# First two token tiles of a two-branch attention kernel: loaded by rows on one DMA queue and turned by TensorE, instead of transposed by DMA

## The chip, the cores and the metric

The kernel runs on one core of one Trainium2 chip (trn2). The metric is the device time of one execution in microseconds (us); 'span' is the part of it from the first to the last instruction in the profile. The kernel before takes 486.67 us (median of 3 runs, 486.44 to 487.22).

## The reference, cut to what matters

```python
def reference(A_x, A_wqkv, A_wo, B_x, B_wqkv, B_wo, gate_w):   # x: [1, 2048, 1024] bf16, wqkv: [1024, 3072]
    def _A_ref(x, wqkv, wo): ...      # linear attention, 32 heads of 32
    def _B_ref(x, wqkv, wo):          # sliding window of 8 keys, dilation 2
        qkv = (x @ wqkv).reshape(B, S, 3, H, Dh) ...
        ...
    x = A_x                           # both branches read the same x
    g = _sigmoid((x * gate_w).sum(-1, keepdims=True))
    return g * _A_ref(x, A_wqkv, A_wo) + (1 - g) * _B_ref(x, B_wqkv, B_wo)
```

The kernel starts with the value projection of branch B: `x @ wqkv[:, 2048:3072]`, a [2048 x 1024] by [1024 x 1024] product. The kernel's matmuls sum over the partitions, in eight blocks of 128 features, so they take x with its features on the partitions, that is, transposed. This document is about the first 16 us, in which that product begins.

## The kernel before

Every operation is recorded with an engine, a guessed cost and a priority. A list scheduler written in Python then fixes the order of each engine's instructions before compilation. Waits are on semaphores, one semaphore for each load. x is cut into 16 token tiles of 128 tokens (256 KB each). The weights of this product come in two halves of 512 columns, each as four "pairs" of 128-row blocks (256 KB a pair).

```python
WARM = 11
...
def load_x(t, prio):                       # DMA transpose: HBM rows -> SBUF, features on partitions
    return P.op("sp", lambda e: e.dma_start_transpose(xT[:, :, t*128:(t+1)*128], x2[e_, r*128:(r+1)*128, :]), 1.5, ...)

def load_w(slot, half, src, c0, prio, d0=0, d1=8, eng="sp", after=()):   # blocks d0..d1 of one half
    return P.op(eng, lambda e: e.dma_start(ws[slot][:, d0:d1, half*512:half*512+512], src[:, d0:d1, c0:c0+512]), ...)

load_x(0, 0)
load_w(0, 0, Bw, 2048, 0.1, 0, 2, "act")   # pairs 1 and 2 on ScalarE's queue
load_w(0, 0, Bw, 2048, 0.2, 2, 4, "act")
load_w(0, 0, Bw, 2048, 0.3, 4, 6)          # pairs 3 and 4 on the sync queue
load_w(0, 0, Bw, 2048, 0.4, 6, 8)
for t in range(1, NT):
    load_x(t, 3 + t)
for d in range(0, 8, 2):                   # the second half
    load_w(0, 1, Bw, 2560, 6.1 + 0.1 * d, d, d + 2)
...
for i in range(WARM):                      # matmuls on zeros, to get TensorE's clock up
    P.op("pe", lambda e: e.matmul(banks[7].ap(), warm[:, 0:128], warm[:, :], start=True, stop=True), 0.43, ..., prio=-1)
...
for t, half in [...]:                      # tiles 0-3 half 1, tiles 0-3 half 2, tiles 4-7 half 1, ...
    step = 2 if t == 0 else 8              # tile 0 waits for its weights pair by pair
    for d in range(0, 8, step):
        o = group(bank, xs, w, [xr, ws[0].part((d, d+step), ...)], d, d + step)   # 8 matmuls 128x512 in all
    move(...)                              # PSUM -> SBUF on ScalarE or VectorE
    P.op("sp", ... e.dma_start(vB_hbm[...], vt[...]) ...)                          # store the values
```

So the early loads come from two queues: tile 0 and pairs 3 and 4 from the sync engine's (SP), pairs 1 and 2 from ScalarE's (ACT).

Of the kernel before, what the change touches and what calls it, by code (L numbers as in the profile page):

```python
# [6 lines left out]
ACT = mybir.ActivationFunctionType  # L7
ALU = mybir.AluOpType
AX = mybir.AxisListType
BF16 = mybir.dt.bfloat16  # L10
# [52 lines left out]
class Prog:  # L63
# [58 lines left out]
    def schedule(self, dma_rate=0.2e6):  # L122
# [6 lines left out]
        dma_free = 0.0  # L129
# [20 lines left out]
        while done < len(self.ops):  # L150
            best = None
            for e in self.ENGS:
                while wait[e] and wait[e][0][0] <= free[e]:
                    _, _, o = heapq.heappop(wait[e])
                    heapq.heappush(avail[e], (o.prio, o.seq, o))
                if avail[e]:
                    t = free[e]
                elif wait[e]:
                    t = wait[e][0][0]
                else:  # L160
                    continue
                if best is None or t < best[0]:
                    best = (t, e)
            assert best is not None, "no operation can go"
            t, e = best
            if not avail[e]:
                while wait[e] and wait[e][0][0] <= t:
                    _, _, o = heapq.heappop(wait[e])
                    heapq.heappush(avail[e], (o.prio, o.seq, o))
            _, _, o = heapq.heappop(avail[e])  # L170
            if e == "pe":

                if o.mode != mode and mode != "m":
                    near = [x for x in avail[e] if x[2].mode == mode and x[0] < o.prio + 30]
                    if near:
                        x = min(near)
                        avail[e].remove(x)
                        heapq.heapify(avail[e])
                        heapq.heappush(avail[e], (o.prio, o.seq, o))
                        o = x[2]  # L180
                if o.mode != mode:
                    t += 0.09
                mode = o.mode
            o.start = t
            o.end = t + o.cost
            free[e] = o.end
            fin = o.end
            if o.chan is not None:
                dma_free = max(dma_free, o.end) + o.lat
                fin = dma_free + o.pad  # L190
            o.pos = len(self.order[e])
            self.order[e].append(o)
            done += 1
            for u in o.users:
                lat = self.LAT[o.eng] if (u.eng != o.eng or o in u.raw) and o.chan is None else 0.0
                if u.eng == o.eng == "pe":
                    lat = 0.0
                ready_at[u] = max(ready_at[u], fin + lat)
                left[u] -= 1
                if left[u] == 0:  # L200
                    ready(u, ready_at[u])
# [915 lines left out]
def build_kernel(nc, A_x, A_wqkv, A_wo, B_x, B_wqkv, B_wo, gate_w, out):  # L1117
    del B_x
    S = A_x.shape[1]
    NT = S // 128  # L1120
    HS = S // 2
    x2 = A_x[0].rearrange("(m e) d -> e m d", e=2)
    out2 = out[0].rearrange("(m e) d -> e m d", e=2)

    base = [(nc.sbuf_base + 31) // 32 * 32]
# [40 lines left out]
    banks = [Bank(i) for i in range(8)]  # L1166
# [51 lines left out]
    warm = SB([128, 512], BF16, "warm", at=pk.t[2].lo)  # L1218
    gwb = SB([128, 1024], BF16, "gwb", at=pk.t[3].lo)
    xn = Ring([SB([128, 1024], BF16, "xn%d" % i, at=az.t[i].lo) for i in range(2)])  # L1220
    top_ = base[0]
    base[0] = ph
    osb = Ring([SB([128, 1024], BF16, "o%d" % i) for i in range(2)])
# [4 lines left out]

    FILL = 0.2
    PVLAG = 3  # L1230
    WARM = 11
    PASSES = 6
    mm = lambda n: max(n / 2400.0, 0.0267) + 0.0025
    act = lambda n: 0.19 + n / 1200.0
# [2 lines left out]
    def plan(seen):  # L1237
# [25 lines left out]
        def C(eng, fn, cost, writes, reads=()):  # L1263
            return P.op(eng, fn, cost, reads=reads, writes=writes, prio=-1)

        for z in vst.t:
            C("pool", lambda e, z=z: e.memset(z[:, :, 32:33], 1.0), 0.1, [z.part((0, 16), (32, 33))])
        C("pool", lambda e: e.memset(eps[:], 1e-6), 0.1, [eps.all()])
        for i, (n, offs) in enumerate(KINDS):
            for h, o in enumerate(offs):  # L1270
                m = mtmp[h]
                b0 = o + 64 * h
                C("pool", lambda e, m=m: e.memset(m[:], 1.0), 0.1, [m.all()])

                C("pool", lambda e, m=m, n=n, b0=b0: e.affine_select(out=m[:, :, 0:n], in_=m[:, :, 0:n], compare_op=ALU.is_ge, fill=0.0, base=b0,
                                                                     pattern=[[0, 2], [1, n]], channel_multiplier=-1), 0.3, [m.all()], [m.all()])
                C("pool", lambda e, m=m, n=n, b0=b0: e.affine_select(out=m[:, :, 0:n], in_=m[:, :, 0:n], compare_op=ALU.is_ge, fill=0.0, base=7 - b0,
                                                                     pattern=[[0, 2], [-1, n]], channel_multiplier=1), 0.3, [m.all()], [m.all()])
                C("dve", lambda e, m=m, n=n, h=h, i=i: e.tensor_copy(msk[i][64 * h:64 * h + 64, :, :], m[64 * h:64 * h + 64, :, 0:n]), 0.2, [msk[i].all()], [m.all()])
                P.ops[-1].prio = 1100  # L1280
        C("pool", lambda e: e.memset(zsel[:], 0.0), 0.3, [zsel.all()])

        C("dve", lambda e: e.memset(warm[:, :], 0.0), 0.15, [warm.all()])
# [29 lines left out]
            return P.op(eng, lambda e: e.dma_start(ws[slot][:, d0:d1, half * 512:half * 512 + 512], src[:, d0:d1, c0:c0 + 512]), 0.4 + 0.2 * n,  # L1313
                        writes=[ws[slot].part((d0, d1), (half * 512, half * 512 + 512))], prio=prio, chan="w%d_%d_%d" % (slot, half, d0), lat=0.55 * n, after=after)

        load_x(0, 0)
        load_w(0, 0, Bw, 2048, 0.1, 0, 2, "act")
        load_w(0, 0, Bw, 2048, 0.2, 2, 4, "act")
        load_w(0, 0, Bw, 2048, 0.3, 4, 6)
        load_w(0, 0, Bw, 2048, 0.4, 6, 8)  # L1320
        for t in range(1, NT):
            load_x(t, 3 + t)
        for d in range(0, 8, 2):
            load_w(0, 1, Bw, 2560, 6.1 + 0.1 * d, d, d + 2)
        P.op("sp", lambda e: e.dma_start(gwb[:, :], gate_w[None, :].to_broadcast([128, D])), 0.6, writes=[gwb.all()], prio=29, chan="gw", lat=0.8)
# [46 lines left out]
        for i in range(WARM):  # L1372
            P.op("pe", lambda e: e.matmul(banks[7].ap(), warm[:, 0:128], warm[:, :], start=True, stop=True), 0.43, reads=[warm.all()], writes=[banks[7].iv], prio=-1)


        early = {(2, 0): (1, 0, Bw, 1024, 21), (4, 1): (2, 0, Bw, 0, 22), (7, 1): (1, 1, Bw, 1536, 23), (10, 1): (2, 1, Bw, 512, 24),
                 (12, 1): (3, 0, Aw, 1024, 25), (14, 1): (3, 1, Aw, 1536, 26)}
        for t, half in [(4 * b + i, half) for b in range(NT // 4) for half in range(2) for i in range(4)]:
            vt, vs = vst.next()
            xs, xr = x_tile(t)  # L1380
            bank = main.next()
            w, wr = w_half(0, half)
            step = 2 if t == 0 else 8
            for d in range(0, 8, step):
                o = group(bank, xs, w, [xr, ws[0].part((d, d + step), (half * 512, half * 512 + 512))], d, d + step)
            move(vt[:, :, 0:32], lambda bank=bank: bank.ap().rearrange("p (h d) -> p h d", d=32), 512, bank, vt.part((0, 16), (0, 32)))
            P.op("sp", lambda e, t=t, vt=vt, half=half: e.dma_start(vB_hbm[t * 128:(t + 1) * 128, half * 528:half * 528 + 528], vt[:, :, :].rearrange("p h d -> p (h d)")), 0.6, reads=[vt.all()],
                 writes=[hb(t * 128, (t + 1) * 128, half)], chan="vst%d" % vs, lat=0.5, prio=5)
            if (t, half) in early:
                load_w(*early[t, half], after=[o])  # L1390
        load_w(0, 0, Aw, 2048, 30)
        load_w(0, 1, Aw, 2560, 31)

# [424 lines left out]
```

## Time and profile before

| what | value | where |
|---|---|---|
| time | 486.67 us | three runs |
| TensorE (PE) busy | 474.2 us of 485.2 (98%) | busy table |
| first real matmul | 5.54 us | timeline |
| waits of PE for loads after it | 0.40, 0.48, 0.16, 0.25 us | timeline, gaps beyond the normal 0.216 us from matmul to matmul |
| last pair of the second half landed | 15.02 us | landings |
| matmul that needs it (the 39th real one) | 15.08 us | its weight load at 15.06; its own record is missing from the trace |

The page of the kernel before, its busy line (engine, busy us, share of the span, instructions) and the chain that ended last by engine:

```profile
PE 474.2 (98%) x4339; PEld 222.8 (46%) x4403; DVE 285.2 (59%) x547; ACT 140.2 (29%) x227; POOL 5.9 (1%) x36
PE 95%; SPq 2%; issue 1%; DMA 1%; ACT 0%; DVE 0%
```

From 15.3 us to the end PE works without a real pause, so whatever the opening loses or gains shows one for one in the time. The timeline of PE in the opening of the kernel before (start, duration, engine, source line, operation, tiles, count, and in brackets the idle time before and who ended it). L1373 are the warm-up matmuls, L1334 the real ones:

```profile
1.25 4.01 PE L1373 MATMUL ps_all<-warm 128*128 128x512 bf16 x11 [1.25 <-DVE warm L1283]
5.54 1.47 PE L1334 MATMUL ps_all<-w,xT 128*128 128x512 bf16 x6 [0.28 <-DMA xT<-in_A_x_dram]
7.25 0.60 PE L1334 MATMUL ps_all<-w,xT 128*128 128x512 bf16 x2 [0.24 <-DMA w<-in_B_wqkv_dram]
8.17 6.82 PE L1334 MATMUL ps_all<-w,xT 128*128 128x512 bf16 x30 [0.32 <-DMA xT<-in_A_x_dram]
15.30 1.89 PE L1334 MATMUL ps_all<-w,xT 128*128 128x512 bf16 x8 [0.30 <-DMA w<-in_B_wqkv_dram]
```

Each break in the row of matmuls is ended by a load. What the loads do is seen in a table by stretch of the kernel before (columns: stretch in us; its length and the busy us of each engine with its instructions; granted clock; mean busy share of the 16 DMA engines, which can pass 1 as packets overlap; GB/s moved):

```profile
2.00:3.00 1.00, 1.00 (x4) 0.36 (x3) 0.63 (x8) 1.00 (x1) 1.00 (x6) 1.00 0.80 245
3.00:4.00 1.00, 1.00 (x4) 0.39 (x3) 0.53 (x3) 0.06 (x1) 0.79 (x5) 1.00 1.16 304
4.00:5.00 1.00, 1.00 (x5) 0.31 (x3) 0.28 (x2) 0.00 (x0) 0.90 (x5) 1.00 1.14 320
5.00:6.00 1.00, 0.72 (x5) 0.23 (x4) 0.21 (x1) 0.00 (x0) 0.89 (x5) 1.00 1.01 298
6.00:7.00 1.00, 1.00 (x5) 0.20 (x3) 0.43 (x2) 0.00 (x0) 0.41 (x2) 1.00 1.18 290
7.00:8.00 1.00, 0.62 (x3) 0.11 (x2) 0.00 (x0) 0.10 (x1) 0.00 (x0) 1.00 1.28 270
8.00:9.00 1.00, 0.83 (x4) 0.41 (x5) 0.00 (x0) 0.50 (x1) 0.00 (x0) 1.00 0.94 213
```

### The profile page before, as it was taken

How to read it: one execution, taken by the hardware profiler on the slowest of the kernel's cores; microseconds unless marked ns; L12 is line 12 of the kernel's file. 1: busy time of each engine (PE TensorE's matmuls, PEld its weight loads, DVE VectorE, ACT ScalarE, POOL GpSimd, SP SyncE). 2: the span in 40 equal slices, each digit the busy share in tenths (PEclk: the TensorE clock that was granted, in tenths of full speed). 3: DMA queues.
4: the chain of work that ended last, by engine and by line, in shares of the span. 5: the costliest groups of instructions: out<-in, count | busy, mean ns of one | idle time of the engine just before them, and what ended most of it. 6: DMA issues, size and time to landing. Idle time of an engine off the chain costs nothing.

```text
span 485.2 us, 10105 instructions
## 1 busy us (share of the span) xinstructions
PE 474.2 (98%) x4339; PEld 222.8 (46%) x4403; DVE 285.2 (59%) x547; ACT 140.2 (29%) x227; POOL 5.9 (1%) x36
## 2 busy tenths in 40 slices
PE   8999999999999999999999999999999999999997
PEld 3444444444444444454544554444444444444443
DVE  2121435888688888665666556496579236653434
ACT  2111121235322234334443333455532230111000
POOL 4000000000000000000000000000000000000000
PEclk9999999999999999999999999999999999999999
DMA  8999993132014459433222322820086018830212
GB/s 224 222 194 299 309 355 122 65 110 86 1 44 135 107 138 245 100 76 86 55 75 67 85 66 66 204 54 2 10 217 163 1 15 242 221 24 2 88 68 89
DMA packets 72951, 57.39 MB, mean 118 GB/s; under 512 B 37953, under 2 KB 60865, under 8 KB 72898
## 3 DMA queue, kind: packets, MB, share of 16 engines
q1 hardware_dynamic: 72210, 56.07, 44.3%
q8 instruction: 36, 0.59, 0.5%
q10 hardware_dynamic: 688, 0.59, 0.4%
q14 instruction: 17, 0.14, 0.1%
HBM read 34.49 MB, written 13.76 MB: 99 GB/s over the span
## 4 chain that ended last, share of the span: by engine, by line
PE 95%; SPq 2%; issue 1%; DMA 1%; ACT 0%; DVE 0%
PE ps_all L1334 78%; PE ps_all L1693 11%; PE ps_all L1463 2%; PE ps_all L1440 2%; SPq L1308 1%; DMA w<-in_B_wqkv_dram 1%; PE ps_all L1556 1%; SPq L1313 1%; PE ps_all L1638 0%; PE ps_all L1610 0%; ACT e L1341 0%; DVE o L1697 0%
## 5 line engine op out<-in xcount | busy, mean ns | idle before, releaser
L1334 PE MATMUL ps_all<-w,xT 128*128 128x512 bf16 x924 | 208.6, 379 | 4.5 <-issue 2.1
L1334 PE MATMUL ps_all<-xT,w 128*128 128x512 bf16 x745 | 166.3, 379 | 2.2 <-issue 1.4
L1334 PEld LDWEIGHTS ps_all<-w,xT 128*128 128x128 bf16 x960 | 91.2, 98 | 111.1 <-DMA w<-in_B_wqkv_dram 2.1
L1334 PEld LDWEIGHTS ps_all<-xT,w 128*128 128x128 bf16 x768 | 73.9, 98 | 88.7 <-issue 1.3
L1693 PE MATMUL ps_all<-w,qT 128*128 128x512 bf16 (+1 forms) x260 | 55.4, 372 | 0.2
L1693 PEld LDWEIGHTS ps_all<-w,qT 128*128 128x128 bf16 x264 | 25.9, 98 | 29.6
L1365 DVE CAST vst<-ps_all 128x512 bf16<-128x512 f32 x15 | 10.4, 694 | 43.5 <-PE ps_all L1334 43.5
L1448 ACT ACTIVATE E<-ps_all 128x1824 bf16<-128x1824 f32 (+1 forms) x18 | 30.4, 1689 | 13.4 <-PE ps_all L1440 13.4
L1345 DVE TENSOR_SCALAR e<-e 128x512 bf16<-128x512 bf16 x64 | 18.4, 290 | 26.9 <-ACT e L1343 14.0
L1697 DVE SCALAR_TENSOR_TENSOR o<-ps_all,gm,xT 128x512 bf16<-128x512 f32 (+1 forms) x25 | 18.0, 728 | 21.1 <-PE ps_all L1693 20.8
L1341 ACT ACTIVATE e<-ps_all 128x512 bf16<-128x512 f32 x32 | 19.1, 598 | 39.0 <-PE ps_all L1334 38.1
L1343 ACT ACTIVATE e<-ps_all 128x512 bf16<-128x512 f32 x32 | 19.1, 598 | 32.3 <-PE ps_all L1334 32.3
L1295 DVE TENSOR_TENSOR mx<-mx,kT 128x1024 bf16<-128x1024 bf16 x32 | 20.9, 688 | 10.9 <-ACT kT L1366 10.8
L1295 DVE TENSOR_TENSOR mx<-mx,qT 128x1024 bf16<-128x1024 bf16 x32 | 20.8, 687 | 7.9 <-ACT qT L1369 7.9
L1451 DVE TENSOR_TENSOR E<-E,msk 128x1824 bf16<-128x1824 bf16 (+1 forms) x18 | 19.9, 1104 | 7.8 <-ACT E L1448 7.4
L1366 ACT ACTIVATE vst<-ps_all 128x512 bf16<-128x512 f32 x17 | 10.2, 601 | 48.5 <-PE ps_all L1334 45.1
L1480 DVE TENSOR_TENSOR ot<-ps_all,rs 128x512 bf16<-128x512 f32 x36 | 23.3, 686 | 0.0
L1366 ACT ACTIVATE az<-ps_all 128x512 bf16<-128x512 f32 x22 | 13.2, 601 | 34.5 <-PE ps_all L1334 34.5
L1366 ACT ACTIVATE kT<-ps_all 128x512 bf16<-128x512 f32 x20 | 11.9, 597 | 37.6 <-PE ps_all L1334 37.6
L1347 DVE SCALAR_TENSOR_TENSOR pk<-ps_all,e 128x512 bf16<-128x512 f32 x32 | 22.0, 689 | 0.7
L1369 ACT ACTIVATE qT<-ps_all 128x512 bf16<-128x512 f32 x19 | 11.4, 598 | 37.4 <-PE ps_all L1334 37.3
L1369 ACT ACTIVATE xT<-ps_all,g 128x512 bf16<-128x512 f32 x10 | 6.9, 689 | 45.1 <-PE ps_all L1334 45.1
(72 smaller groups left out, 260.2 us busy)
## 6 DMA issues: line engine op xcount, KB each, us to landing
rb<-rc_hbm SPq DMA_DIRECT2D x32, 256.0 KB, 5.2
w<-in_A_wqkv_dram SPq DMA_DIRECT2D x6, 1024.0 KB, 9.0
v<-vB_hbm SPq DMA_DIRECT2D x36, 132.0 KB, 2.7
vB_hbm<-vst SPq DMA_DIRECT2D x32, 132.0 KB, 6.2
w<-in_B_wqkv_dram SPq DMA_DIRECT2D x4, 1024.0 KB, 9.5
xn<-in_A_x_dram SPq DMA_DIRECT2D x16, 256.0 KB, 2.7
out_dram<-o SPq DMA_DIRECT2D x15, 256.0 KB, 2.1
oB_hbm<-ot SPq DMA_DIRECT2D x36, 96.0 KB, 2.2
```

The lines of the kernel that those rows point to most:

```text
L1295: P.op("dve", lambda e, m=m, op=op: e.tensor_tensor(m[:, 0:n], m[:, 0:n], src, op), 0.08 + n / 1920.0, reads=[m.all(), reg], writes=[m.all()],
L1334: last = e.matmul(bank.ap(), lhs(dc), rhs(dc), start=(dc == 0), stop=(dc == 7))
L1341: P.op("act", lambda e: e.activation(e_[:, :], bank.ap(), ACT.Exp), act(512), reads=[bank.iv], writes=[e_.all()])
L1343: P.op("act", lambda e: e.activation(e_[:, :], bank.ap(), ACT.Exp, accum_out=qe[:, col:col + 1]), act(512) + 0.1, reads=[bank.iv], writes= ...
L1345: P.op("dve", lambda e: e.tensor_scalar(e_[:, :], e_[:, :], 1.0, 1e-6, op0=ALU.min, op1=ALU.add), 0.25, reads=[e_.all()], writes=[e_.all()])
L1347: P.op("dve", lambda e: e.scalar_tensor_tensor(out=dst, in0=bank.ap(), scalar=0.0, in1=e_[:, :], op0=ALU.max, op1=ALU.add), dps(512), read ...
L1366: fa = lambda e: e.activation(dst, src(), ACT.Copy)
L1369: fa = lambda e: e.activation(dst, src(), ACT.Copy, scale=scale)
L1448: P.op("act", lambda e: e.activation(E[:, 0:32 * nq].rearrange("p (j q) -> p j q", j=4), ps[:, 4:8, 0:8 * nq], ACT.Exp), act(32 * nq), rea ...
L1451: P.op("dve", lambda e: e.tensor_tensor(ev(), ev(), m[:, :, :].rearrange("p r q -> p (r q)")[:, None, :].to_broadcast([128, 16, 2 * nq]), ...
L1480: P.op("dve", lambda e, r=r, bv=bv, h=h: e.tensor_tensor(o[:, 512 * h:512 * h + 512].rearrange("p (k i c) -> p k i c", k=2, c=32), bv()[:, ...
L1693: last = e.matmul(bank.ap(0, f1 - f0), qT[:, dc, t * 128:(t + 1) * 128], ws[3][:, dc, f0:f1], start=(dc == 0), stop=(dc == 7))
```

## The change

Its intent is to start real work sooner. The first two DMA transposes took the sync engine 1.38 and 1.25 us to issue and landed 4.7 and 4.8 us after their issue began. The change loads the first two tiles as plain rows, in order of need with the weight pairs, all on the sync queue. TensorE turns them with an identity matrix into PSUM, and VectorE and ScalarE copy them to where the transposes would have put them. Five warm-up matmuls go (eleven become four plus two), because the turns keep PE busy too, and the building of the masks moves behind the first projections.

```diff
+    rows_ = [SB([128, 1024], BF16, "rows%d" % i, at=az.t[2 + i].lo) for i in range(2)]
+    ident = SB([128, 128], BF16, "ident", at=er.t[0].lo)
-    WARM = 11
+    WARM = 4
+    WARM2 = 2
@@ the masks: built with priority -1 at the start before, now recorded after the projections @@
@@ the loads @@
-        load_x(0, 0)
-        load_w(0, 0, Bw, 2048, 0.1, 0, 2, "act")
-        load_w(0, 0, Bw, 2048, 0.2, 2, 4, "act")
-        load_w(0, 0, Bw, 2048, 0.3, 4, 6)
-        load_w(0, 0, Bw, 2048, 0.4, 6, 8)
-        for t in range(1, NT):
-            load_x(t, 3 + t)
+        due(load_rows(0, 0, 512, 0), 0.4, 2.0)            # due(load, issue cost, guessed landing): for the scheduler
+        due(load_w(0, 0, Bw, 2048, 0.1, 0, 2), 0.45, 2.7)
+        due(load_rows(0, 512, 1024, 0.2), 0.45, 3.1)
+        due(load_w(0, 0, Bw, 2048, 0.3, 2, 4), 0.45, 3.9)
+        due(load_rows(1, 0, 1024, 0.4), 0.45, 4.7)
+        due(load_w(0, 0, Bw, 2048, 0.5, 4, 6), 0.45, 5.5)
+        due(load_w(0, 0, Bw, 2048, 0.6, 6, 8), 0.45, 6.3)
+        for t in range(2, NT):
+            o = load_x(t, 3 + t)
@@ after the warm-ups @@
+        for t, p in [(t, p) for t in range(2) for p in range(4)]:
+            b = banks[3 + p]
+            def turn(e, t=t, b=b, p=p):
+                for k in range(2):
+                    d = 2 * p + k
+                    last = e.matmul(b.ap(128 * k, 128 * k + 128), rows_[t][:, d * 128:(d + 1) * 128], ident[:, :], start=(k == 0), stop=(k == 1), skip_group_check=True)
+                return last
+            P.op("pe", turn, 0.22, ...)
+            ...                                           # then a copy 128x256 to xT, VectorE for even p, ScalarE for odd p
+        for i in range(WARM2):
+            P.op("pe", ...)                               # two more warm-ups, as before
-            step = 2 if t == 0 else 8
+            step = 2 if t == 0 or t == 1 and half == 0 else 8
```

(Cuts are marked with "..." and "@@".) The lists of instructions, compared engine by engine, show that PE's order differs only in the opening. On the sync queue the fourth pair of the second half now comes after the first store.

More of the change, by code (lines that the diff above doesn't have):

```diff
@@ L188, in schedule @@
             if o.chan is not None:
-                dma_free = max(dma_free, o.end) + o.lat
-                fin = dma_free + o.pad
+                if o.lat is None:
+                    fin = max(o.end + 1.2, o.pad)
+                else:
+                    dma_free = max(dma_free, o.end) + o.lat
+                    fin = dma_free + o.pad
             o.pos = len(self.order[e])
@@ L1264, in C @@
             return P.op(eng, fn, cost, reads=reads, writes=writes, prio=-1)
+        C("pool", lambda e: e.memset(ident[:, :], 0.0), 0.1, [ident.all()])
+        C("pool", lambda e: e.affine_select(out=ident[:, :], in_=ident[:, :], compare_op=ALU.not_equal, fill=1.0, base=0, pattern=[[-1, 128]], channel_multiplier=1), 0.3,
+          [ident.all()], [ident.all()])
         for z in vst.t:
@@ L1268, in plan @@
         C("pool", lambda e: e.memset(eps[:], 1e-6), 0.1, [eps.all()])
-        for i, (n, offs) in enumerate(KINDS):
-            for h, o in enumerate(offs):
-                m = mtmp[h]
-                b0 = o + 64 * h
-                C("pool", lambda e, m=m: e.memset(m[:], 1.0), 0.1, [m.all()])
-                C("pool", lambda e, m=m, n=n, b0=b0: e.affine_select(out=m[:, :, 0:n], in_=m[:, :, 0:n], compare_op=ALU.is_ge, fill=0.0, base=b0,
-                                                                     pattern=[[0, 2], [1, n]], channel_multiplier=-1), 0.3, [m.all()], [m.all()])
-                C("pool", lambda e, m=m, n=n, b0=b0: e.affine_select(out=m[:, :, 0:n], in_=m[:, :, 0:n], compare_op=ALU.is_ge, fill=0.0, base=7 - b0,
-                                                                     pattern=[[0, 2], [-1, n]], channel_multiplier=1), 0.3, [m.all()], [m.all()])
-                C("dve", lambda e, m=m, n=n, h=h, i=i: e.tensor_copy(msk[i][64 * h:64 * h + 64, :, :], m[64 * h:64 * h + 64, :, 0:n]), 0.2, [msk[i].all()], [m.all()])
-                P.ops[-1].prio = 1100
         C("pool", lambda e: e.memset(zsel[:], 0.0), 0.3, [zsel.all()])
@@ L1314, in load_w, with load_rows, due @@
                         writes=[ws[slot].part((d0, d1), (half * 512, half * 512 + 512))], prio=prio, chan="w%d_%d_%d" % (slot, half, d0), lat=0.55 * n, after=after)
-        load_x(0, 0)
-        load_w(0, 0, Bw, 2048, 0.1, 0, 2, "act")
-        load_w(0, 0, Bw, 2048, 0.2, 2, 4, "act")
-        load_w(0, 0, Bw, 2048, 0.3, 4, 6)
-        load_w(0, 0, Bw, 2048, 0.4, 6, 8)
-        for t in range(1, NT):
-            load_x(t, 3 + t)
+        def load_rows(t, lo, hi, prio):
+            return P.op("sp", lambda e: e.dma_start(rows_[t][:, lo:hi], x2[0, t * 128:(t + 1) * 128, lo:hi]), 0.45, writes=[rows_[t].part((lo, hi))], prio=prio, chan="xr%d_%d" % (t, lo))
+        def due(o, cost, at):
+            o.cost, o.lat, o.pad = cost, None, at
+        due(load_rows(0, 0, 512, 0), 0.4, 2.0)
[7 more added lines that the diff above has]
+            o = load_x(t, 3 + t)
+            if t < 4:
+                due(o, 1.4, 7.6 + 1.3 * (t - 2))
         for d in range(0, 8, 2):
@@ L1373, in plan @@
             P.op("pe", lambda e: e.matmul(banks[7].ap(), warm[:, 0:128], warm[:, :], start=True, stop=True), 0.43, reads=[warm.all()], writes=[banks[7].iv], prio=-1)
+        for t, p in [(t, p) for t in range(2) for p in range(4)]:
[5 more added lines that the diff above has]
+                return last
+            P.op("pe", turn, 0.22, reads=[rows_[t].part((256 * p, 256 * p + 256)), ident.all()], writes=[b.iv], prio=-0.5 + 0.01 * p)
+            src = lambda b=b: b.ap(0, 256).rearrange("p (k s) -> p k s", k=2)
+            dst = xT[:, 2 * p:2 * p + 2, t * 128:(t + 1) * 128]
+            fn = (lambda e, dst=dst, src=src: e.activation(dst, src(), ACT.Copy)) if p % 2 else (lambda e, dst=dst, src=src: e.tensor_copy(dst, src()))
+            P.op("act" if p % 2 else "dve", fn, act(256) if p % 2 else dps(256), reads=[b.iv], writes=[xT.part((2 * p, 2 * p + 2), (t * 128, (t + 1) * 128))], prio=3 + 0.01 * p)
+        for i in range(WARM2):
+            P.op("pe", lambda e: e.matmul(banks[7].ap(), warm[:, 0:128], warm[:, :], start=True, stop=True), 0.43, reads=[warm.all()], writes=[banks[7].iv], prio=-0.4)
         early = {(2, 0): (1, 0, Bw, 1024, 21), (4, 1): (2, 0, Bw, 0, 22), (7, 1): (1, 1, Bw, 1536, 23), (10, 1): (2, 1, Bw, 512, 24),
@@ L1382, in plan @@
             w, wr = w_half(0, half)
-            step = 2 if t == 0 else 8
+            step = 2 if t == 0 or t == 1 and half == 0 else 8
             for d in range(0, 8, step):
-                o = group(bank, xs, w, [xr, ws[0].part((d, d + step), (half * 512, half * 512 + 512))], d, d + step)
+                o = group(bank, xs, w, [xT.part((d, d + step), (t * 128, (t + 1) * 128)), ws[0].part((d, d + step), (half * 512, half * 512 + 512))], d, d + step)
             move(vt[:, :, 0:32], lambda bank=bank: bank.ap().rearrange("p (h d) -> p h d", d=32), 512, bank, vt.part((0, 16), (0, 32)))
@@ L1390, in plan @@
                 load_w(*early[t, half], after=[o])
+        for i, (n, offs) in enumerate(KINDS):
+            for h, o in enumerate(offs):
+                m = mtmp[h]
+                b0 = o + 64 * h
+                P.op("pool", lambda e, m=m: e.memset(m[:], 1.0), 0.1, writes=[m.all()])
+                P.op("pool", lambda e, m=m, n=n, b0=b0: e.affine_select(out=m[:, :, 0:n], in_=m[:, :, 0:n], compare_op=ALU.is_ge, fill=0.0, base=b0,
+                                                                     pattern=[[0, 2], [1, n]], channel_multiplier=-1), 0.3, writes=[m.all()], reads=[m.all()])
+                P.op("pool", lambda e, m=m, n=n, b0=b0: e.affine_select(out=m[:, :, 0:n], in_=m[:, :, 0:n], compare_op=ALU.is_ge, fill=0.0, base=7 - b0,
+                                                                     pattern=[[0, 2], [-1, n]], channel_multiplier=1), 0.3, writes=[m.all()], reads=[m.all()])
+                P.op("dve", lambda e, m=m, n=n, h=h, i=i: e.tensor_copy(msk[i][64 * h:64 * h + 64, :, :], m[64 * h:64 * h + 64, :, 0:n]), 0.2, writes=[msk[i].all()], reads=[m.all()])
         load_w(0, 0, Aw, 2048, 30)
```

## The prediction

> **What bounds the kernel now.** TensorE. The busy table gives PE 474.2 of 485.2 us (98%) and the chain of waits is 95% PE. From 15.3 us on the chain is an almost unbroken row of 128x512 matmuls, one per 0.216 us. PE's instruction list in the changed kernel differs only in the opening, so only the first 15 us should change.
>
> **The opening now (timeline, DMA landings).** 11 warm-up matmuls on PE from 1.25 to 5.26 us. The first real matmul starts at 5.54, when the first transposed token tile lands (issued 0.80, landed 5.49; its first weight pair, on the other queue, landed 3.58). Then PE waits 0.40 us for the fourth weight pair (landed 7.21), 0.48 for tile 1 (8.13), and about 0.4 in all for the last two pairs of the second weight half (14.34 and 15.02). That is 1.3 us of stalls after 5.54. The DMA runs near 300 GB/s in 3 to 9.5 us, with a hole around 9.5 to 10.3 us because the sync queue was still issuing transposes (1.25 to 2.27 us each) and gave out the second half only at 8.31 to 10.4.
>
> **What the change does.** Two transposes (1.38 + 1.25 us of queue time) become three plain loads (about 0.5 us each); the two weight issues of the ScalarE queue move to the sync queue. 16 128x128 matmuls and 8 copies of 128x256 (estimate 0.4 us each, from 0.69/0.60 us for 128x512) are added; PE loses five warm-up matmuls.  The bytes to load are the same, so the supply still sets the pace: I estimate (0.8 to 0.9 us per 256 KB, from the old landings) half a row tile at 3.1 us, weight pairs at about 3.7, 4.9, 6.4, 7.4, tiles 2 and 3 at 8.5 and 9.6.
>
> First real matmul: 4.6 to 5.0 us. Tiles 0 and 1 share each weight pair, so when the fourth pair lands at about 7.4 only 8 matmuls remain: done at 9.2, against 10.1 for the first two tiles before. Then 22 matmuls lead to the last pair of half two at about 14.0, where before it was reached at 15.06. That pair is now issued after the first store, at about 10 us as before, so it lands at 13.5 to 14.5 and may itself take back some of the gain. All of that is on the critical path: a gain of 0.3 to 1.3 us.
>
> **Against it.** The Trainium skill ("TensorE: Matmul & The Clock Gate", Part 1) says that the clock opens only after about 3.4 us of activity, judged in a free-running window. The trace agrees: warm-ups 0.427 us apart up to 4.2 us, then 0.216. With four plus two warm-ups and gaps, the clock may open a window later (about 7.6 us); I estimate that this would cost at most 0.8 us.
>
> **Prediction.** 485.9 us, 0.8 us less than 486.67; 8 in 10 between 485.0 and 486.9. Faster by over 2%: 0.01; within 2%: 0.97; slower by over 2%: 0.02.
>
> **What would show it.** Timeline: first 128x512 matmul of weights at 4.6 to 5.0 us. Waits: the wait for tile 1 gone, waits for weight pairs early instead. Chain: unbroken PE from about 14 us instead of 15.3, with the same 470 us from there to the end. Landings: fourth pair near 7.4 us, last pair of half two before 14.5.
>
> **What would make it wrong.** The last pair of the second half landing at 15 us again (store and queue in front of it): no gain. The clock staying at half rate past 7.6 us. The fourth pair at 8 us or later. A changed split of evictions between VectorE and ScalarE that makes PE wait in the middle.

## The result, and the profile after

| | median us | range | runs |
|---|---|---|---|
| before | 486.81 | 486.44 to 487.22 | 6 |
| changed | 488.55 | 487.89 to 489.98 | 6 |

The ratio is 1.004, with a 95% interval from 1.0023 to 1.0057. Ratios here are the mean time of one kernel's fast runs over that of the other's fast runs of the same rounds, so not quite the ratio of the medians quoted. The class "within 2%" was right, but the change made the kernel slower by about 1.8 us where a gain of 0.8 was predicted, outside the stated range. Three things stand out: the changed kernel is slower, it scatters more (2.1 us against 0.8), and its time outside the span is longer (2.11 us on average against 1.74).

The same lines of the page of the changed kernel:

```profile
PE 480.4 (99%) x4414; PEld 223.5 (46%) x4414; DVE 289.0 (59%) x556; ACT 138.0 (28%) x226; POOL 6.3 (1%) x38
PE 98%; DMA 1%; SPq 0%; DVE 0%; issue 0%
```

PE's higher share is no better use: its busy time is 6.2 us longer for the same real work. (Part of that is only that fewer matmul records are missing from this trace.) The timeline of PE in the opening of the changed kernel (L1380 and L1397 warm-ups, L1389 turns, L1341 real matmuls):

```profile
1.25 1.89 PE L1380 MATMUL ps_all<-warm 128*128 128x512 bf16 x4 [1.25 <-DVE warm L1280]
3.07 0.59 PE L1389 MATMUL ps_all<-ident,rows 128*128 128x128 bf16 x4
3.45 1.06 PE L1397 MATMUL ps_all<-warm 128*128 128x512 bf16 x2
5.01 0.61 PE L1389 MATMUL ps_all<-ident,rows 128*128 128x128 bf16 x4 [0.50 <-DMA rows<-in_A_x_dram]
5.41 0.85 PE L1341 MATMUL ps_all<-w,xT 128*128 128x512 bf16 x2
6.54 0.59 PE L1341 MATMUL ps_all<-w,xT 128*128 128x512 bf16 x2 [0.28 <-DMA w<-in_B_wqkv_dram]
7.43 0.62 PE L1389 MATMUL ps_all<-ident,rows 128*128 128x128 bf16 x8 [0.30 <-DMA rows<-in_A_x_dram]
8.52 8.81 PE L1341 MATMUL ps_all<-w,xT 128*128 128x512 bf16 x40 [0.47 <-DMA w<-in_B_wqkv_dram]
```

The first real matmul comes only 0.13 us earlier than before (5.41). Only four real matmuls are done by 8.5 us, where the kernel before had started its tenth. From 8.52 on the row is unbroken and the 39th real matmul starts at 15.87 us, 0.79 us later than before; the span is 0.8 us longer (486.0). So in this execution the whole loss within the span happened before 8.52 us. The chain of waits of the changed kernel's first 16 us names the load behind it (start, duration, what):

```profile
2.70 0.47 SPq L1314
3.17 0.04 issue
3.21 5.27 DMA w<-in_B_wqkv_dram
8.48 0.05 issue
8.52 7.51 PE ps_all L1341 x34
```

It is the third weight pair: issued at 3.21, landed at 8.48. The stretches of the changed kernel:

```profile
2.00:3.00 1.00, 1.00 (x3) 0.15 (x1) 0.63 (x8) 0.09 (x1) 1.00 (x6) 1.00 0.59 179
3.00:4.00 1.00, 1.00 (x7) 0.56 (x6) 0.57 (x3) 0.30 (x1) 0.36 (x2) 1.00 0.87 304
4.00:5.00 1.00, 0.51 (x2) 0.00 (x0) 0.27 (x2) 0.08 (x1) 0.84 (x5) 1.00 0.66 183
5.00:6.00 1.00, 0.99 (x6) 0.56 (x6) 0.53 (x2) 0.34 (x1) 0.74 (x4) 1.00 0.84 272
6.00:7.00 1.00, 0.72 (x4) 0.13 (x2) 0.09 (x1) 0.04 (x1) 0.48 (x2) 1.00 0.93 305
7.00:8.00 1.00, 0.70 (x9) 0.45 (x8) 0.24 (x1) 0.13 (x1) 0.00 (x0) 1.00 1.07 273
8.00:9.00 1.00, 0.53 (x4) 0.24 (x4) 0.81 (x4) 0.53 (x2) 0.53 (x4) 1.00 1.08 160
```

Now the DMA engines idle a third of the time between 4 and 5 us (busy share 0.66, 183 GB/s), although the sync engine had issued all four pairs and both tiles by 4.16 us. In the seven stretches 1.68 MB are moved, against 1.94 before. So the loads are slower although no DMA transpose runs among them until 7 us.

A load is one semaphore raised 16 times. The Trainium skill ("DMA: Bandwidth & Descriptors", section "Why a DMA increments its semaphore by 16 and not by 1") explains that up to 16 DMA engines work on it and finish independently, and that only the full 16 mean that all data are there. This trace agrees: it holds 16 landings for each load, and in the changed kernel they lie far apart. Landing of the first and the last of the 16, in us (computed from the trace's landings; P1 to P4 are the pairs of the first half):

```
              before            changed          predicted (last)
tile 0     5.38 .. 5.49      2.53 .. 2.94 (half), 4.05 .. 4.97     3.1 (half)
P1         3.48 .. 3.58      3.68 .. 4.56          3.7
P2         5.06 .. 5.30      4.71 .. 6.41          4.9
tile 1     7.95 .. 8.13      6.02 .. 7.39
P3         6.16 .. 6.36      6.75 .. 8.48          6.4
P4         7.01 .. 7.21      7.41 .. 9.21          7.4
```

For the four pairs the first engine is close to the prediction, within 0.35 us (P4: 7.41 against 7.4). The last one, which alone counts, is 0.9 to 2.1 us later than predicted. In these loads of the kernel before, the first and the last lay within 0.25 us of each other.

### The profile page after: what moved, and what is told of

Its sections match the earlier page's. It is cut to its first block, busy times and chain, and to the rows that moved or that the text cites. A ratio compares the mean times of both kernels' runs of the same rounds, so it can differ in the third digit from the quotient of the medians.

```text
span 486.0 us, 10198 instructions
## 1 busy us (share of the span) xinstructions
PE 480.4 (99%) x4414; PEld 223.5 (46%) x4414; DVE 289.0 (59%) x556; ACT 138.0 (28%) x226; POOL 6.3 (1%) x38
## 4 chain that ended last, share of the span: by engine, by line
PE 98%; DMA 1%; SPq 0%; DVE 0%; issue 0%
PE ps_all L1341 80%; PE ps_all L1728 11%; PE ps_all L1498 2%; PE ps_all L1475 2%; DMA w<-in_B_wqkv_dram 1%; PE ps_all L1591 1%; PE ps_all L1673 0%; PE ps_all L1645 0%; SPq L1314 0%; SPq L1310 0%; DVE o L1732 0%
## 5 line engine op out<-in xcount | busy, mean ns | idle before, releaser
L1341 PE MATMUL ps_all<-w,xT 128*128 128x512 bf16 x960 | 213.1, 380 | 0.8 <-DMA w<-in_B_wqkv_dram 0.8
L1341 PE MATMUL ps_all<-xT,w 128*128 128x512 bf16 x768 | 169.0, 379 | 0.0
L1341 PEld LDWEIGHTS ps_all<-w,xT 128*128 128x128 bf16 x960 | 91.6, 98 | 109.7 <-ACT xT L1394 0.9
L1341 PEld LDWEIGHTS ps_all<-xT,w 128*128 128x128 bf16 x768 | 73.8, 98 | 88.8 <-issue 1.3
L1373 ACT ACTIVATE kT<-ps_all 128x512 bf16<-128x512 f32 x17 | 10.1, 597 | 37.2 <-PE ps_all L1341 37.1
L1465 DVE TENSOR_SCALAR qd<-qT,par 128x912 bf16<-128x912 bf16 (+1 forms) x34 | 14.6, 451 | 9.5 <-PE ps_all L1475 9.5
```

The lines of the kernel that those rows point to most:

```text
L1341: last = e.matmul(bank.ap(), lhs(dc), rhs(dc), start=(dc == 0), stop=(dc == 7))
L1373: fa = lambda e: e.activation(dst, src(), ACT.Copy)
```

## The experiments

The theories at the start were these. S: plain row loads, with no transpose between them, let the 16 engines run apart, whichever queue issues them. Q: it is the single issuing queue, as the kernel before used two. M: the moved masks get in the way of the turn copies on VectorE. C: fewer warm-ups leave TensorE's clock low for longer. Each run is set against runs of the kernel before in the same rounds; different sets of rounds ran on different chips and are compared only through these. (The expectations call the 16 engines of a load its "rings".)

### e1: two queues again

```diff
-        due(load_w(0, 0, Bw, 2048, 0.1, 0, 2), 0.45, 2.7)
+        due(load_w(0, 0, Bw, 2048, 0.1, 0, 2, "act"), 0.45, 2.7)
-        due(load_w(0, 0, Bw, 2048, 0.3, 2, 4), 0.45, 3.9)
+        due(load_w(0, 0, Bw, 2048, 0.3, 2, 4, "act"), 0.45, 3.9)
```

(The scheduler also moves the fourth pair of the second half ahead of the first store, as the sync queue is freer, and a few evictions near 60 us between ScalarE and VectorE.)

> The changed kernel with its first two weight pairs issued again on ScalarE's queue (rows stay on the sync queue). Theory S (row loads on one queue let the 16 rings of a load run apart, and PE waits for the slowest ring; what decides is plain loads without a transpose between them): spread between first and last ring of the fourth pair stays above 1 us, last ring after 8.4 us, time within 0.5 us of the changed kernel (488.5). Rival Q (the single issuing queue alone is the cause): third and fourth pair complete at 7.2 to 7.8 us, spread under 0.5 us, time 486.0 to 486.9.

Measured: 486.83 us (486.42 to 486.91), ratio to before 0.9993 (0.9979 to 1.0006). P3 landed at 6.26 .. 7.15 and P4 at 7.76 .. 7.92. The timeline of PE of e1, its last two lines before 17 us:

```profile
7.10 0.61 PE L1389 MATMUL ps_all<-ident,rows 128*128 128x128 bf16 x8
7.55 9.66 PE L1341 MATMUL ps_all<-w,xT 128*128 128x512 bf16 x43
```

The unbroken row starts at 7.55 instead of 8.52. Stretches of e1:

```profile
4.00:5.00 1.00, 1.00 (x4) 0.14 (x2) 0.78 (x3) 0.38 (x1) 0.29 (x2) 1.00 1.02 343
8.00:9.00 1.00, 1.00 (x6) 0.47 (x5) 0.73 (x3) 0.18 (x1) 0.81 (x5) 1.00 1.29 259
```

The holes are gone: 343 and 259 GB/s where the changed kernel had 183 and 160. Q's times came out, and S fell in its strong form. Q had expected a spread under 0.5 us, though, and P3 still had 0.9.

One rival was never separated from Q. A single engine issues its loads one after the other, so on one queue they are also issued later. The sync engine's issues in the changed kernel, and then those of the sync engine and of ScalarE in e1:

```profile
2.22 0.43 SPq L1310 DMA_DIRECT2D w<-in_B_wqkv_dram  x1
3.21 0.95 SPq L1310 DMA_DIRECT2D w<-in_B_wqkv_dram  x2
```

```profile
2.19 0.95 SPq L1310 DMA_DIRECT2D w<-in_B_wqkv_dram  x2
0.81 0.98 ACTq L1310 DMA_DIRECT2D w<-in_B_wqkv_dram  x2
```

P3 was issued at 3.21 in the changed kernel and at 2.19 in e1, so 1.02 us of the 1.33 by which it landed later (8.48 against 7.15) may be the later issue alone. From the start of the issue to the last landing the two kernels hardly differ: P2 4.19 us against 4.43, tile 1 4.69 against 4.64, P3 5.27 against 4.96, P4 5.52 against 5.25. Against issue time as the whole cause stands that tile 1 and P3 had been issued by 3.64 when the DMA engines of the changed kernel idled from 4 to 5 us. In all the runs below the two go together: with two queues the last pair of the first half had been issued by 2.80 to 3.31 us, with one by 4.16 to 4.33. So e1 and e2 show what moving two issues costs, and not whether the queue or the later issue is the reason.

### e2: the kernel before with one queue

```diff
-        load_w(0, 0, Bw, 2048, 0.1, 0, 2, "act")
-        load_w(0, 0, Bw, 2048, 0.2, 2, 4, "act")
+        load_w(0, 0, Bw, 2048, 0.1, 0, 2)
+        load_w(0, 0, Bw, 2048, 0.2, 2, 4)
```

> The kernel before with its first two weight pairs moved from ScalarE's queue to the sync queue, behind the first transpose; nothing else. Theory S: rings stay together behind the transpose (spread under 0.5 us for the four pairs), time rises only by the later issue, under 0.6 us. Rival Q: the one queue costs it most of what the change costs, plus 1.2 to 2 us.

Measured: 488.74 us (488.40 to 489.23), ratio 1.0036 (1.0022 to 1.0049). Moving two issues from one queue to the other, and nothing else of the change, costs as much as the whole change did. The timeline of PE of e2:

```profile
1.25 3.83 PE L1373 MATMUL ps_all<-warm 128*128 128x512 bf16 x11 [1.25 <-DVE warm L1283]
6.85 1.95 PE L1334 MATMUL ps_all<-w,xT 128*128 128x512 bf16 x6 [1.76 <-DMA w<-in_B_wqkv_dram]
```

The first real matmul waits for P1, which landed 5.20 .. 6.80 instead of 3.48 .. 3.58. Stretches of e2:

```profile
2.00:3.00 1.00, 1.00 (x4) 0.37 (x3) 0.63 (x8) 0.08 (x1) 1.00 (x6) 1.00 0.93 129
3.00:4.00 1.00, 1.00 (x4) 0.39 (x3) 0.53 (x3) 0.00 (x0) 0.79 (x5) 1.00 0.91 166
```

With the transpose alone in the early queue the DMA moves 129 and 166 GB/s where before had 245 and 304 with two queues. Here the pairs also queue up behind the transpose and are issued later (P1 at 2.23 instead of 0.80, P3 at 3.35 instead of 2.24), so this run shows the price of one queue in the kernel before; it does not show the same hole as in the changed kernel. From issue to last landing the pairs took longer too (P3 4.80 us instead of 4.12), so later issue is not all of it here.

### e3: the masks early again

The edit puts the block that builds the masks back to its old place and priority.

> The changed kernel with the masks built at the start as before. Theories S and Q: same as the changed kernel within 0.4 us (488.2 to 488.9). Rival M (mask copies moved between the turn copies on VectorE delay the opening): 0.5 us or more faster.

Measured: 489.00 us (488.08 to 489.31), ratio 1.0040. That is the changed kernel again (0.1 us above the range of 488.2 to 488.9). M is out.

### e4: eight warm-ups

```diff
-  P.op("pe", lambda e: e.matmul(banks[7].ap(), warm[:, 0:128], warm[:, :], ...), 0.43, ..., prio=-1)
+  P.op("pe", lambda e: [e.matmul(banks[7].ap(), warm[:, 0:128], warm[:, :], ...) for _ in range(2)][-1], 0.43, ..., prio=-1)
   # and the two in the middle write 64 columns only
```

The recorded costs stay, so every other order is the same.

> The changed kernel with eight warm-up matmuls instead of four in front (until about 4.7 us) and the two in the middle cut to 64 columns; all else in the same order. Theories S and Q: same within 0.4 us, as PE waits for loads from 5 to 8.5 us anyway. Rival C (the clock opens late because of fewer warm-ups): at least 0.5 us faster.

Measured: 487.93 us (487.57 to 488.67), ratio 1.0018. On the means of the same rounds that is 0.85 us less than e3 (488.01 against 488.86), which has the changed kernel's opening and its few warm-ups. So C is not out, against what was expected: the warm-ups matter. The spans tell how: e4's lie between 485.5 and 486.5, the changed kernel's between 485.8 and 487.9. The profiled execution of the changed kernel (486.0) was one of its good ones and hides this.

### e14: the kernel before with four warm-ups

```diff
-  P.op("pe", lambda e: e.matmul(banks[7].ap(), warm[:, 0:128], warm[:, :], ...), ...)
+  P.op("pe", lambda e, i=i: e.matmul(banks[7].ap(0, 512 if i < 4 else 32), warm[:, 0:128], warm[:, 0:512 if i < 4 else 32], ...), ...)
```

> The kernel before with only four of its eleven warm-up matmuls at full width; the other seven keep 32 columns, so every order is the same and PE idles from about 3.2 to 5.5 us. Theory C (fewer warm-ups by themselves cost time, by a clock that opens one or two windows of 3.4 us later): clock opens after 5.6 us, 0.4 to 1.2 us slower on the mean and a wider spread of the runs than before's 0.8 us. If the warm-ups do not matter: within 0.3 us of before.

Measured: 488.00 us (487.81 to 488.86), ratio 1.0026 (1.0013 to 1.0040). The spread was not wider than before's, but the 1.2 us are there. The timeline of PE of e14:

```profile
1.25 2.07 PE L1373 MATMUL ps_all<-warm 128*128 128x512 bf16 x11 [1.25 <-DVE warm L1283]
5.68 11.51 PE L1334 MATMUL ps_all<-w,xT 128*128 128x512 bf16 x42 [2.35 <-DMA xT<-in_A_x_dram]
```

The loads are as before (P4 landed at 7.18), and yet 42 real matmuls take 11.5 us: the trace has them 0.427 us apart until 9.9 us, and 0.216 after that. The weight loads of e14 show the change of pace, one in 0.41 us and then 33 in 7.00:

```profile
9.49 0.15 PEld L1334 LDWEIGHTS ps_all<-w,xT 128*128 128x128 bf16 x1 [0.28 <-issue]
9.90 7.00 PEld L1334 LDWEIGHTS ps_all<-w,xT 128*128 128x128 bf16 x33 [0.26 <-issue]
```

When the full clock began in each profiled execution, in us from the start (read from the trace's clock records):

```
eleven warm-ups: before 4.24  e2 3.90
ten:             e17 4.32  e16 5.84
eight:           e13 4.46  e11 4.45  e5 5.21  e4 5.25
four to six:     changed 5.91  e3 5.64  e10 5.74  e15 5.64  e12 5.75  e1 7.06  e6 9.61  e8 10.38  e14 9.87
```

The Trainium skill ("TensorE: Matmul & The Clock Gate", Part 1) says that the clock is judged in windows of 3.413 us that run free of the kernel. The trace agrees: the stretch at full clock lasted either 481.279 or 477.866 us in all the profiled executions listed here but one (e2, 484.693), which are 141, 140 and 142 times 3.413. A window need not be busy from end to end: the clock opened 2.99 us after PE's first matmul (1.25) in the kernel before and 2.65 us after it in e2. With 11 warm-ups PE is busy for 4.0 us on end; with four plus two, a gap may fall into the window that counts, and then another 3.4 us go by. e8 and e6 are read here as such executions; that it was the gap is inferred from when they opened. The page adds that the ramp is below 1% of a typical kernel's span; here it is 0.25% (1.2 us, e14), which agrees, and it is still more than the 0.8 us that the change was to win.

### e8: the transposes issued later

The sync queue waits, before the first transpose, until PE has turned the last part of tile 0. Only this wait is added.

```diff
+        for o, waits in plan["sp"]:
+            if o is self.x2:                    # the transpose of tile 2
+                waits.append(self.t3.val)       # the last turn of tile 0
```

> The changed kernel with the sync queue made to wait, before it issues the first transpose, for PE to have turned the last part of tile 0 (about 5.5 us instead of 4.2); all orders the same. Rival H (generating the transposes' descriptors from 4.2 us on starves the plain loads in flight, the hole of 4 to 5 us): DMA rate in 4 to 5 us rises from 183 to over 280 GB/s and the third pair lands before 7.8 us. Theory Q: the hole stays (160 to 280 GB/s), third pair at 8.0 to 8.7 us; the tile after it lands later, time the same or up to 1 us worse.

Measured: 488.59 us (487.54 to 489.19), ratio 1.0029. The first transpose was issued at 5.13 instead of 4.20, and the hole stayed; P3 landed at 6.63 .. 8.12. The stretch of e8:

```profile
4.00:5.00 1.00, 1.00 (x7) 0.51 (x6) 0.38 (x3) 0.12 (x1) 0.80 (x4) 1.00 0.51 158
```

Rival H is out.

### e6: rows on ScalarE's queue, weights on the sync queue

```diff
 def load_rows(t, lo, hi, prio):
-            return P.op("sp", ...
+            return P.op("act", ...
```

> The changed kernel with the three row loads on ScalarE's queue and all weight pairs on the sync queue. Theory Q (two issuing queues keep more of the 16 rings busy, whichever load is on which): as with the weights moved, 486.4 to 487.1, third pair landed by 7.5 us. Rival W (it was the weight pairs themselves that had to come off the queue that also carries transposes): stays at 488 or more.

Measured: 487.93 us (487.12 to 488.55), ratio 1.0019 (1.0006 to 1.0032), so neither side's number. The stretch of e6:

```profile
4.00:5.00 1.00, 0.93 (x6) 0.60 (x7) 0.52 (x2) 0.30 (x1) 0.00 (x0) 1.00 1.08 341
```

The loads did what Q said (341 GB/s in 4 to 5 us, P3 at 6.64 .. 7.43), but PE's row ran at half clock until 9.6 us in the profiled execution: ScalarE's first row load landed at 3.94, the turns began at 4.07, and PE was idle for 0.9 us before them. So good loads do not seem to help when the clock is late: the run lost 0.9 us, of which about 0.26 is its longer time outside the span (2.00 against 1.74). The profiled execution was the slowest of the five (488.55), so the clock of the others is not known.

### e12: all plain loads on ScalarE's queue

All seven plain loads move to ScalarE's queue. The transposes stay on the sync queue, held back as in e8. PE's order differs a little, so only the loads are compared (one look).

> A look at the loads only: all seven plain loads on ScalarE's queue, the transposes alone on the sync queue and held until tile 0 is turned. Theory Q (one queue of plain loads leaves rings idle, whichever engine issues): a hole under 250 GB/s in the stretch from 4 to 5 us as in the changed kernel (183), third pair landed after 7.8 us. Rival P (it belongs to the sync queue): over 300 GB/s there, third pair by 7.4 us. PE's order differs a little, so its time is not compared.

Measured: 487.71 us (one run). The stretch of e12:

```profile
4.00:5.00 1.00, 0.66 (x4) 0.13 (x3) 0.28 (x2) 0.76 (x1) 0.82 (x5) 1.00 0.80 202
```

The hole is there on ScalarE's queue too, and P3 landed at 6.58 .. 8.28. It belongs to one queue (and one issuing engine) that carries everything, not to the sync queue: the last pair had been issued by 4.21 us here, as late as in the changed kernel.

All profiled executions together, the MB moved from 2 to 9 us (the sum of the seven stretches of each):

```
one queue carries the early loads                         two queues
e2 1.53  changed 1.68  e4 1.69  e13 1.70  e3 1.71         e16 1.81  before 1.94  e17 1.95  e6 1.96
e10 1.71  e12 1.71  e8 1.78  e15 1.78                     e14 1.96  e5 2.02  e1 2.04  e11 2.04
```

No one-queue run reaches any two-queue run, though e16, in which one engine lagged, comes close to the best of them. (e10 and e13 have one tiny load on the second queue; they count as one.) Why one queue leaves engines idle, after its loads have been issued, was not settled: the trace shows the idle time, and nothing of what the queue waits for.

### e10: a tiny load on ScalarE's queue

```diff
+        P.op("act", lambda e: e.dma_start(xn.t[0][:, 0:16], x2[0, 0:128, 0:16]), 0.4, ..., prio=-2, chan="touch", lat=0.1)
```

> The changed kernel with one tiny load (32 bytes a partition, nobody reads it) issued first on ScalarE's queue. The time outside the profile's span is 2.1 us in the changed kernel and 1.75 before. If that extra 0.35 us is due to ScalarE's queue being first used at the very end: outside time falls to about 1.8 us, span unchanged within 0.5, so about 0.3 us faster. If not: 2.1 us stays.

Measured: 487.80 us (487.00 to 488.08), ratio 1.0017. The time outside the span fell from 2.11 to 1.76 us, as expected. The spans were 485.2 to 486.3, on the mean 485.9 against 486.7 of the changed kernel, where no change beyond 0.5 was expected: long executions like that of 487.9 did not come up in these five runs. Whether that is chance, no run tells.

### e13: eight warm-ups and the tiny load

Both edits together, still with all early loads that matter on the sync queue.

> The changed kernel, still with all loads on the sync queue, with eight warm-ups and the tiny load on ScalarE's queue together. If the parts add (clock 0.8 us, outside time 0.35 us), 487.3 to 487.6, so that 0.5 to 0.8 us against before stays for the single queue. If it falls to 486.9 or less, the single queue costs nothing on its own in this kernel.

Measured: 487.46 us (486.95 to 488.03), ratio 1.0011 (0.9998 to 1.0025). That lies in the range expected if the parts add up: 0.58 us on the means stay against before (487.52 against 486.94), which the expectation puts down to the single queue (less what the earlier rows may win). It is a remainder that is not clear of noise: the interval reaches from -0.1 to 1.2 us. And e10, with few warm-ups, lay only 0.8 us above before (487.70 against 486.89), so that the parts add up is not shown.

### e15: an extra ScalarE instruction

```diff
+        C("act", lambda e: e.activation(qe[:, 0:1], eps[:, :], ACT.Copy), 0.2, [qe.part((0, 1))], [eps.all()])
```

> The changed kernel with one extra one-column copy on ScalarE after its table load, no DMA there. If the time outside the span hangs on ScalarE's DMA queue being used early: it stays at 2.1 us. If it hangs on something like the length or place of the instruction stream, which any extra instruction shifts: it changes (1.75 as with the tiny load). The span is expected at 485.8 to 487.9 as in the changed kernel.

Measured: 487.91 us (487.80 to 490.27), ratio 1.0038. The time outside the span stayed at 2.10 to 2.17. So it is not just any instruction. But it is not just the first use of the queue either:

```
early loads on ScalarE's queue and time outside the span (mean, us)
none: changed 2.11, e3 2.10, e4 2.13, e8 2.13, e15 2.12, e2 1.97     one: e10 1.76, e13 1.74
two: before 1.74, e14 1.74, e1 1.81, e5 1.82, e17 1.83     three: e6 2.00     four: e11 2.10, e16 2.10     seven: e12 1.71
```

What makes it 1.7 or 2.1 stays open. It is in the time of a run and in no profile, and it was worth 0.37 us of the loss.

### e5, e11, e16, e17: is there a version that beats both?

e5 is e1 with eight warm-ups. e11 has rows on the sync queue, P1 and P2 on ScalarE's, P3 and P4 split over both, eight warm-ups, and an order in which PE uses tile 1 with the first two pairs before the third comes:

```diff
+        due(load_rows(0, 0, 512, 0), 0.4, 2.2)
+        due(load_w(0, 0, Bw, 2048, 0.1, 0, 2, "act"), 0.45, 3.2)
+        due(load_rows(0, 512, 1024, 0.2), 0.45, 3.1)
+        due(load_w(0, 0, Bw, 2048, 0.3, 2, 4, "act"), 0.45, 4.9)
+        due(load_rows(1, 0, 1024, 0.4), 0.45, 4.9)
+        due(load_w(0, 0, Bw, 2048, 0.5, 4, 5), 0.45, 6.7)
+        due(load_w(0, 0, Bw, 2048, 0.5, 5, 6, "act"), 0.45, 6.7)
+        due(load_w(0, 0, Bw, 2048, 0.6, 6, 7), 0.45, 7.3)
+        due(load_w(0, 0, Bw, 2048, 0.6, 7, 8, "act"), 0.45, 7.3)
```

e16 and e17 are e11 and e5 with ten warm-ups and the extra ScalarE copy.

> The two-queue form of the changed kernel (weight pairs 1 and 2 on ScalarE's queue) with eight warm-up matmuls in front, so that the clock is open when its first real matmuls come at 5.4 us (in the two-queue run they still came 0.427 us apart until 7.1). Expected, if PE's clock is what holds that form now: unbroken matmuls from about 7.15 us instead of 7.55 and 0.3 to 0.6 us less, 486.2 to 486.5. If the loads hold it: no change against 486.8.

> The best version that the theories suggest: rows on the sync queue, weight pairs 1 and 2 on ScalarE's, pairs 3 and 4 split over both, eight warm-ups, PE's order so that tile 1 uses the first two pairs while it waits for the third. Expected: unbroken matmuls to the point where before had its last wait 0.5 to 0.9 us earlier than before, 485.9 to 486.4 us, against 486.8 before. If the loads, and not PE's order, hold the two-queue form: 486.6 to 486.9.

> The balanced version with ten warm-up matmuls (to about 5.5 us; before has eleven) and the same extra copy. Its spans were 484.8, 484.9, 484.9, 485.7, 485.7 with eight; if the two longer ones came from a late clock, all lie at 484.7 to 485.2 now. Time 486.5 to 486.9 if the time outside falls to 1.75, else 486.9 to 487.2.

> The two-queue form with ten warm-ups and the extra copy. Spans were 484.6 to 485.1 and once 486.3 with eight; expected 484.6 to 485.1 throughout, 486.3 to 486.8 us, so 0.1 to 0.5 us less than before, perhaps not to be told from it.

| | median us | ratio to before (95%) | spans |
|---|---|---|---|
| e5 | 486.72 | 1.0001 (0.9989 to 1.0013) | 484.6 to 486.3 |
| e11 | 487.03 | 1.0010 (0.9997 to 1.0024) | 484.8 to 485.7 |
| e16 | 487.30 | 1.0005 (0.9991 to 1.0019) | 484.6 to 486.3 |
| e17 | 487.05 | 1.0005 (0.9992 to 1.0019) | 485.0 to 485.5 |

None beats the kernel before by more than the runs scatter, and the hoped-for 0.3 to 0.9 us came in no time. In e5 the profile does show part of the gain. Its last line of PE in the opening:

```profile
7.31 9.89 PE L1341 MATMUL ps_all<-w,xT 128*128 128x512 bf16 x45 [0.25 <-DMA w<-in_B_wqkv_dram]
```

With 34 more matmuls at 0.216 us, the 39th real one starts at about 14.65 us (7.31 + 34 x 0.216), some 0.4 us before the 15.08 of the kernel before. In the time, 0.1 of that goes to the longer time outside the span (1.82 against 1.73); the rest is within the scatter. In e16 the ten warm-ups did not narrow the spans: in its profiled execution one of the 16 engines was late from the load of tile 1 on (5.53 .. 7.74), whatever the clock did.

## Why the prediction was wrong

- "On the critical path: the opening" was right. PE's order is the same after it, and the 0.8 us that the profiled span lost are the 0.79 us that the 39th real matmul came later.
- "The bytes to load are the same, so the supply still sets the pace", at "0.8 to 0.9 us per 256 KB, from the old landings", is the step that failed. Loads did set PE's pace, but not at the old rate: 1.68 MB came in 2 to 9 us instead of 1.94, with the DMA engines idle for a third of 4 to 5 us. The old landings had been delivered by two queues. On one queue the pairs' last landings came 0.9 us (P1) to 2.1 us (P3, the load that PE waited for: 8.48 us, not 6.4) after the predicted times. e1 and e2 show that the move of two issues from ScalarE's queue makes the difference: undoing it gives the changed kernel some 2 us back (ratio 1.0040 to 0.9993), and making it alone costs the kernel before 1.8 (about 0.2 of that outside the span). How much of it is the queue and how much the issue of P3 at 3.21 us instead of 2.19 (e1) is open. The prediction had counted the move as nothing but two more issues, and had not put even their time into the landings.
- "The clock may open a window later; at most 0.8 us" was named as a risk and left out of the expected time. e4 against e3 puts it at 0.85 us on the mean, and e14 shows 1.2 us in the kernel before. It comes in some executions only, hence the scatter.
- The time outside the span (0.37 us) was not foreseen, and its cause is open.
- A tally of the three, 0.37 outside, 0.85 clock and 0.6 queue (e13), makes 1.8 us, about what was lost (1.7 on the medians, 1.95 on the means). It is no proof, as the queue's part is a remainder with zero in its interval, and it is net of whatever the earlier rows win, which no run shows by itself. e1, which has few warm-ups too, shows that the parts are not independent: with good loads its five runs lost nothing against before.
- "First real matmul at 4.6 to 5.0" failed in the profiled execution: the second half of tile 0 landed at 4.97, and the first real matmul came at 5.41. It was not what decided: in e3, e8, e10 and e15, with the same loads, this half landed by 4.34 to 4.45, the first real matmul came at 4.80 to 4.90, and PE then waited for P2 (landed 6.24 to 6.71). "Fourth pair at 8 us or later" was listed as what would make the prediction wrong, and that is what happened.
- "The last pair of the second half landing at 15 us again" came true as well: it landed at 15.63 us, not at 13.5 to 14.5. It cost nothing only because PE was late itself and came to it at 15.87; PE on the predicted schedule (14.0) would have had to wait for it if it had still landed then. The moved masks cost nothing (e3).

## What to carry to other kernels

Before you move a DMA issue from one engine's queue to another, look at when the last early load will be issued and at how much the early loads move in all. Here two queues had issued their pairs by 3.31 us and moved 1.81 to 2.04 MB between 2 and 9 us; one queue had issued them by 4.33 at the latest and moved 1.53 to 1.78. Plan with the landing of the last of a load's engines, and take it from a stretch with the same queues as the new design. Warm-up work that looks idle may hold the clock: when you trade it for useful work with gaps, one profiled execution will not show the price, but the spread of several runs will.

## What the Trainium skill lacked or had wrong

- "DMA: Bandwidth & Descriptors", section "Issuing engines are not separate DMA queues", says that issuing from several engines "will only save the time on the sequencer", and that this time is usually small beside the DMA itself. Here it was not small: P3 was issued 1.02 us later on one queue than in e1. Whether that is all, as the page says, no run settles. P3 landed 1.33 us later, and one queue moved 183 GB/s in 4 to 5 us where e1 moved 343; over 2 to 9 us the nine one-queue profiles moved 1.53 to 1.78 MB, seven of the eight two-queue ones 1.94 to 2.04 and the eighth 1.81. It cost 1.8 us in a kernel of 487 (e2).
- The same page tells that a load's engines finish independently, but gives no size for how far apart. Here first and last lay 0.1 to 0.25 us apart for the early loads of the kernel before and up to 1.7 us apart for plain loads on one queue (P2 and P3 of the changed kernel).
- No page that I read says what a DMA transpose does behind engines that have run apart. In the changed kernel the transpose's 256-byte packets that started early all ended together: those started at 7.82, 8.26, 8.46, 8.54 and 8.76 us took 1.23, 0.80, 0.60, 0.52 and 0.31 us, and so ended at 9.05 to 9.07. In e2 they ended at 8.68 to 8.72 in the same way. That the transpose waits there for the slowest engine is an inference from these times. Ten of P4's 16 landings came together just after it, at 9.06 to 9.21, though its last 1 KB packet had ended at 8.87; so part of P4's lateness may belong to the transpose behind it.
- "TensorE: Matmul & The Clock Gate", Part 1, was right about the window (stretches at full clock of 140 to 142 times 3.413 us). It was also right that the ramp is below 1% of a kernel (0.25% here), but it does not say that this can outweigh a small change: four warm-ups instead of eleven cost 1.2 us (e14).
- No page that was found tells why the time outside the profile's span differs from kernel to kernel. It was 1.7 to 2.1 us here and nearly constant for each kernel.
